# Sketch attention and a squared-relu layer on one core: the first batch's order, the loads of v, and what stands behind x on the queue

## The chip, the core and the metric

The kernel runs on one core of a Trainium2 chip. The core has a matrix engine (TensorE, PE in the profile, its weight loads PEld), VectorE (DVE), ScalarE (ACT), GpSimd (POOL) and SyncE (SP), which issues nearly all the DMAs. The metric is the device time of one execution in microseconds. Beside it stands the span of a profiled execution, from its first to its last instruction.

## The reference

```python
# q, k, v: (4, 4, 1088, 32) float32; S1, S2: (8, 32)
def phi(x):                                  # 64 features: products of two sketches
    a = np.einsum('rd,bhsd->bhsr', S1, x)
    b = np.einsum('rd,bhsd->bhsr', S2, x)
    return np.einsum('bhsi,bhsj->bhsij', a, b).reshape(*x.shape[:-1], 64)
q_p, k_p = phi(q), phi(k)
kv  = np.einsum('bhsf,bhsd->bhfd', k_p, v)   # per head 64 x 32
z   = np.sum(k_p, axis=2)
num = np.einsum('bhsf,bhfd->bhsd', q_p, kv)
den = np.einsum('bhsf,bhf->bhs', q_p, z)[..., None] + 1e-06
x   = (num / den).transpose(0, 2, 1, 3).reshape(4352, 128)
out = np.maximum(x @ w_in, 0)**2 @ w_out     # 128 -> 2048 -> 128, float32 out
```

## The kernel before, in words

The Python code records the instructions of every engine in an order that it fixes itself (a manual schedule); each engine then runs its list in that order, and semaphores make it wait for data and for free buffers.

**Layout.** A batch has 4 heads of 1088 rows. A partition holds 34 consecutive rows of one head: two groups g of 16 rows, and a remainder of 2. A group of a batch is a chunk of 512 tokens for the feed-forward part; there are 8 such chunks and one of 256 tokens for the remainders.

**Feed-forward part.** For each chunk there are 16 blocks: `first_product` (L938) multiplies x, turned (xT, f16), with 128 columns of w_in into a tile pg; relu and square go over VectorE and ScalarE, or ScalarE and POOL (gt, g2); `block` (L1026) multiplies g2 with w_out, adding up in a tile po. The first product is made three blocks ahead. pg has two buffers, so the next pg waits until the relu of the one before last has read it. `first_two` (L968) makes the first two blocks of the first chunk by hand. A finished po is turned, scaled by beta and stored in four pieces by SP (L918).

**Attention.** Rows of k and q are turned in squares of 32 (`turned`, L242) and multiplied with a block-diagonal sketch matrix w_bd (`proj`, L257); `outer` (L344) forms the 64 features. `KvRows` adds up v and k features (`values`, L433) and, from the two factors, the sums z (`factor_sums`, L389); `turn` and `place` (L479, L487) and `own_sums` (L409, L416) spread both over a block-diagonal kvbd. `numerators` (L257, tile nd) multiplies turned q features with kvbd; `normalize` divides, scales each token by its largest value, and keeps the scale for beta. xT comes either over TensorE (x_ps) or, where there is time, over DRAM: SP writes x (L643), waits until it has landed, and reads it back in four pieces (L649).

**The first batch** is written out by hand from L1035 to the end of the setup: seven idle products, which keep TensorE active, the sketch's turn s_ps, four small idle products, then projections, features, sums, values, numerators, normalisation and the first products.

**The later batches** run as generators (`batch_gen`) that are advanced between blocks; a counter of blocks (`now`) and planned costs of VectorE and POOL decide when each continues. For them the features of q come from factors that go over DRAM: `factors_gen` issues q_one (L299), two q_two (L304), and, when these have landed, the two loads of f (L313, L316); POOL multiplies them (phF, L326), and nd waits for phF. `chunk_of` sends beta over DRAM too: SP writes it (L663) and, when it has landed, reads it as beta_t (L664). SP is one queue: a DMA that waits holds up all that stand behind it.

**Loads.** SP issues, in this order, the two k groups of the first batch, k's remainder, q's first group, v by head (four loads of 128 KB over 128 partitions), q's second group, v's remainder (v_rm, two loads, L131), then the weights and the second batch. S1 and S2 come from ScalarE's queue.

Of the kernel before, what the change touches and what calls it, by code (L numbers as in the profile page):

```python
# [8 lines left out]
F32 = mybir.dt.float32  # L9
# [12 lines left out]
def kernel(  # L22
# [24 lines left out]
    VONE = H * 8 * D  # L47
# [33 lines left out]
    for b in range(B):  # L81
        for x, tag in ((k_sb, "k_sb"), (q_sb, "q_sb")):
            x[b] = cpool.tile([128, NM * D], F32, name=f"{tag}{b}")
        v_sb[b] = cpool.tile([128, VONE + D], F32, name=f"v_sb{b}")
    for r in range(2):
        v_rm[r] = cpool.tile([128, H * D + D], F32, name=f"v_rm{r}")
# [33 lines left out]
    def load_v(b, h):  # L120
        sp.dma_start(  # L121
            v_sb[b][:, 256 * h : 256 * h + 256],
            bass.AP(
                v.tensor,
                v.offset + (b * H + h) * S * D,
                [[NM * D, 32], [8 * D, 4], [1, 8 * D]],
            ),
        )

    def load_v_rest(b, i):  # L130
        sp.dma_start(  # L131
            _v(v_rm[b // 2], 0, [[D, H], [1, D]], 64 * (b % 2) + 32 * i, 32),
            bass.AP(
                v.tensor,
                v.offset + (b * H * S + 32 + i) * D,
                [[NM * D, 32], [S * D, H], [1, D]],
            ),
        )
# [26 lines left out]
    load_k(0, 1)  # L165
    load_rest(k_sb[0], k, 0)
    load_q(0, 0)
    for h in range(H):
        load_v(0, h)
    load_q(0, 1)  # L170
    for i in range(2):
        load_v_rest(0, i)
# [7 lines left out]
    for i in range(2):  # L180
        load_v_rest(1, i)
# [14 lines left out]
    for h in range(H):  # L196
        dve.memset(own[32 * h : 32 * h + 32, h : h + 1], 1.0)
    w_bd = cpool.tile([128, H * 16], F32)
# [4 lines left out]
    for i in range(B):  # L203
        (dve if i == 0 else pool).memset(kvbd[i][:], 0.0)
    for b in range(B):
        pool.memset(v_sb[b][:, VONE : VONE + D], 1.0)
    for r in range(2):
        pool.memset(v_rm[r][:, H * D : H * D + D], 1.0)
# [19 lines left out]
    def idle_products(n, w=512):  # L228
        idle_ps = pspool.tile([128, 512], F32, name="idle_ps", tag="po", bufs=2)
        for i in range(n):  # L230
            nc.tensor.matmul(idle_ps[:, 0:w], zero[:, 0:128], zero[:, 0:w])  # L231
# [5 lines left out]
    def turned(x, g, of_q=False):  # L237

        if g < 2:
            xt = apool.tile([128, 512], F32, tag="xt", bufs=6)  # L240
            c0, w = (512 * g, 128) if of_q else (128 * g, 256)
            dve.transpose(  # L242
                xt[:, :] if of_q else _v(xt, 0, [[128, 4], [1, 4], [4, 32]]),
                _v(x, c0, [[32, 4], [w, 4], [1, 32]]),
            )
        else:
            xt = apool.tile([128, 64], F32, tag="xtr", bufs=4)
            if of_q:
                dve.transpose(_v(xt, 0, [[1, 2], [2, 32]]), _v(x, 1024, [[32, 2], [1, 32]]))
            else:  # L250
                dve.transpose(xt[:, :], x[:, 1024:1088])
        return xt
# [32 lines left out]
    def factors_gen(b, qf, w, fs):  # L285


        for g in range(2):


            n, p0 = 2 * w[g], 64 * g
            one = dpool.tile([16, n], F32, name=f"q_one{b}{g}", tag=f"q_one{b}{g}")
# [61 lines left out]
    rest_ab = {}  # L354
    for r in range(2):
        rest_ab[r] = (
            cpool.tile([128, 64], F32, name=f"abr{r}"),
            cpool.tile([128, 256], F32, name=f"phr_k{r}"),
        )

    def proj_rests(xk, b, xqs, qf=None, ps_tag="ms"):


        ab_ps = pspool.tile([128, 128], F32, name="abr_ps", tag=ps_tag, bufs=2)
        p0 = 64 * (b % 2)
        tiled(ab_ps, 0, 64, xk, 0, w_bd[:, :], 64, p0)
        for g, xt in xqs:
            nc.tensor.matmul(ab_ps[64 * g : 64 * g + 64, 64:128], w_bt[:, :], xt[:, 0:64])
        act.copy(
            _v(rest_ab[b // 2][0], 0, [[32, 2], [8, 4], [1, 8]], p0, 64),  # L370
            _v(ab_ps, 0, [[8, 2], [16, 4], [1, 8]], p0, 64),
        )
        for g, _ in xqs:
            act.copy(qf[64 * g : 64 * g + 64, 512:576], ab_ps[64 * g : 64 * g + 64, 64:128])
        return ab_ps

    def outer_rest(b, eng, a=None):
        p0 = 64 * (b % 2)
        ab, ph = rest_ab[b // 2]
        eng.tensor_tensor(  # L380
            out=_v(ph, 0, [[64, 4], [8, 8], [1, 8]], p0, 64),
            in0=_v(ab if a is None else a, 0, [[8 if a is None else 16, 4], [1, 8], [0, 8]], p0, 64),
            in1=_v(ab, 32, [[8, 4], [0, 8], [1, 8]], p0, 64),
            op=mult,
        )

    def factor_sums(ps, c0, ab, a0, a1, w, p0, n, first, last):

        nc.tensor.matmul(  # L389
            ps[32 * w : 32 * w + 32, c0 : c0 + 32],  # L390
            ab[p0 : p0 + n, a0 : a0 + 32],
            ab[p0 : p0 + n, a0 + a1 : a0 + a1 + 32],
# [30 lines left out]
    class KvRows:  # L423
# [3 lines left out]
        def __init__(self, b, abs_=None):  # L427
            self.b, self.abs = b, abs_
            self.ps = pspool.tile([128, 1024], F32, name="kvr_ps", tag="nd", bufs=1)

        def values(self, ph, c0, vt, v0, v1, p0, n, first, last):
            for h in range(H):
                nc.tensor.matmul(  # L433
                    self.ps[32 * h : 32 * h + 32, 0:64],
                    vt[p0 : p0 + n, v0 + v1 * h : v0 + v1 * h + 32],
                    ph[p0 : p0 + n, c0 + 64 * h : c0 + 64 * h + 64],
# [4 lines left out]
        def tile(self, ph, g, t, last=False):  # L441
            self.values(
                ph, 256 * t, v_sb[self.b], D * (4 * g + t), 256, 0, 128, g + t == 0, last
            )

        def rest(self, last=False):
            r, p0 = self.b // 2, 64 * (self.b % 2)
            self.values(rest_ab[r][1], 0, v_rm[r], 0, D, p0, 64, False, last)

        def rest_sums(self):  # L450
            factor_sums(
                self.ps, 512, rest_ab[self.b // 2][0], 0, 32, 0, 64 * (self.b % 2), 64, False, True
            )
# [5 lines left out]
        def keep_sums(self):  # L459
            self.sums = apool.tile([128, 32], F32, name="kvz", tag="kvz")  # L460
            act.copy(self.sums[:, :], self.ps[:, 512:544])

        def products(self, phs):
            for g in range(2):
                for t in range(4):
                    self.tile(phs[g], g, t)
                for t in range(4):
                    factor_sums(
                        self.ps, 512, self.abs, 128 * g + 32 * t, 256, t, 0, 128,
                        g == 0, g == 1 and t > 0,  # L470
                    )
            self.rest(True)
# [19 lines left out]
        def spread(self):  # L492
# [4 lines left out]
            own_sums(self.b, t_ps, 64)  # L497
# [34 lines left out]
    def normalize_first(nds, xT):  # L532


        (den, rden, top, rtop, rs), (_, mp, _, beta) = norm_tiles()
        xs = apool.tile([128, 512], F16, tag="xs")
        for i, nd in enumerate(nds):
# [10 lines left out]
        dve.tensor_tensor(out=rtop[:, :], in0=top[:, :], in1=rden[:, :], op=mult)  # L548

        mm, rm = (_v(nds[1], 144 + 8 * x, [[1, 4]]) for x in range(2))  # L550
        dve.tensor_reduce(
            out=mm, in_=_v(rtop, 0, [[4, 4], [1, 4]]),
            axis=AX, op=amax, apply_absolute_value=True,
        )
        dve.tensor_scalar(
            out=mp[:, :], in0=mm, scalar1=1.0, scalar2=1.0 / 1024.0, op0=add, op1=mult,
        )
        dve.reciprocal(rm, mp[:, :])
        dve.tensor_tensor(
            out=_v(rs, 0, [[4, 4], [1, 4]]),  # L560
            in0=_v(rden, 0, [[4, 4], [1, 4]]),
            in1=_v(nds[1], 152, [[1, 4], [0, 4]]),
            op=mult,
# [8 lines left out]
        yield  # L572
        pool.tensor_tensor(out=beta[:, :], in0=mp[:, :], in1=mp[:, :], op=mult)
# [13 lines left out]
    def normalize(nd, T, xT, col, chunk):  # L587
# [59 lines left out]
        yield 3, 0  # L647
# [32 lines left out]
    nd_taken = [False]  # L680
    ms_until = [0]
# [73 lines left out]
    def batch_gen(b):  # L755
# [55 lines left out]
        kv.spread()  # L811
# [223 lines left out]
    idle_products(7)  # L1035
    s_ps = pspool.tile([128, 16], F32, name="s_ps", tag="nd", bufs=1)
    nc.tensor.transpose(s_ps[:, :], s_nat[:, :], iden[0:16, 0:16])
    idle_products(4, 128)
    xk = [turned(k_sb[0], 0)]
# [5 lines left out]
    )  # L1045
    for x in range(2):
# [5 lines left out]
    pk = [proj(xk[0], "pg"), proj(xk[1], "pg")]  # L1052
    phk = [ph_tile("ph_k", 3) for g in range(2)]
    phq = ph_tile("ph_q", 2)
    xkr = turned(k_sb[0], 2)
    xq = turned(q_sb[0], 0, True)
    for g in range(2):
        outer(phk[g], pk[g][1], 0, 2, dve, pk[g][0])
        outer(phk[g], pk[g][1], 2, 2, pool)
    pq = proj(xq, "po")  # L1060
    pkr = proj_rests(xkr, 0, [])
    kv0 = KvRows(0)
    for g in range(2):
        for t in range(4):
            factor_sums(kv0.ps, 512, pk[g][1], 32 * t, 128, t, 0, 128, g == 0, g == 1 and t > 0)
# [9 lines left out]
    pick_sums(zt_ps, 0, kv0.sums)  # L1075
    for t in range(4):
        kv0.tile(phk[1], 1, t)
    own_sums(0, zt_ps, 0)
    xq1 = turned(q_sb[0], 1, True)
# [17 lines left out]
    kv0.rest(True)  # L1097
    kv0.keep_rows()
    pqT = [turned_half(phq, 0, (act, act))]
# [3 lines left out]
    pqT.append(turned_half(phq, 2, (act, dve)))  # L1103
# [5 lines left out]
    pq1 = proj(xq1, "pg")  # L1109
    phq1 = ph_tile("ph_q", 2)  # L1110
    xT0 = apool.tile([128, 512], F16, name="xT", tag="xT", bufs=3)
    norm = normalize_first(nd0, xT0)
    next(norm)
    for t0 in (0, 2):
        outer(phq1, pq1[1], t0, 2, pool)
# [4 lines left out]
    idle_products(4)  # L1120
    chunk_of(0, 0, xT0, next(norm))
    first_two()
    pqT = [turned_half(phq1, 0, (act, dve))]
# [10 lines left out]
    def second_group():  # L1134
        pqT.append(turned_half(phq1, 2, (act, dve)))
        yield 1, 0
# [6 lines left out]
    lanes.append([second_group(), 1, 1])  # L1143
    add_work(*(batch_gen(b) for b in range(1, B)))
    later = []
    for b in range(2, B):
# [4 lines left out]
        later += [(n + 6 + i, load_v_rest, (b, i)) for i in range(2)]  # L1151
# [40 lines left out]
```

## Time and profile before

| what | value |
|---|---|
| three runs | 196.22, 196.79, 197.50 us; median 196.79 |
| the profiled execution | 196.73 us, span 194.8 us, granted TensorE clock 1.000 |
| TensorE busy | 185.4 us (95% of the span) |
| VectorE, ScalarE, POOL busy | 119.6, 108.2, 71.1 us |
| first idle product | 1.19 us |
| first values (L433) | 8.69 us |
| first pg (L968) | 18.10 us |
| DMA, main queue | 22.86 MB, 45.2% of 16 engines' span |

A line of the timeline reads: start in us from the span's start, length in us, engine, line, operation, output<-input, shapes, count, and in brackets how long the engine was idle before it and what ended that. A q behind an engine's name (SPq) means its queue of DMA issues. A line of the chain of work that ended last reads: start, length, what. `issue` is time in which an engine waited for nothing that the profile shows.

### The profile page before, as it was taken

Reading aid. Unit: us, or ns where it says so; the run is one execution under the profiler, and the core shown is the slowest. Engines: PE = TensorE matmul, PEld = TensorE weight load, DVE = VectorE, ACT = ScalarE, POOL = GpSimd, SP = SyncE. Lnnn points to the kernel's source line nnn. Section 1 sums busy time; section 2 is a strip of 40 time slices with the busy share of each in tenths; the row PEclk is TensorE's granted clock in tenths of the full one; section 3 lists DMA queues with packets and bytes.
Section 4 is the critical chain, followed back from the end, with each engine's and each line's share of the span. In section 5 each row is a group of like instructions: output and inputs, shape, how many; then the busy total and the mean of one; then the engine's idle time right before and its main releaser. Section 6 shows DMA issues by size and latency. Waiting matters only on the chain.

```text
span 194.8 us, 3746 instructions
## 1 busy us (share of the span) xinstructions
PE 185.4 (95%) x1380; PEld 97.2 (50%) x1380; DVE 119.6 (61%) x272; ACT 108.2 (56%) x212; POOL 71.1 (36%) x91
## 2 busy tenths in 40 slices
PE   7985999999999999999999999999999999999992
PEld 2763445454545454545454455554454444444791
DVE  4956495556487848455877545567558664644671
ACT  3235659655466755544766655457646565456570
POOL 3604122645236229242370654542524222522200
PEclk9999999999999999999999999999999999999999
DMA  6799380298913837649130349199100411300021
GB/s 170 212 347 313 107 298 25 59 242 279 228 16 108 253 69 177 192 94 280 27 54 1 52 96 263 42 227 231 29 3 0 84 30 13 54 0 2 5 52 27
DMA packets 37826, 23.17 MB, mean 119 GB/s; under 512 B 27888, under 2 KB 33264, under 8 KB 37808
## 3 DMA queue, kind: packets, MB, share of 16 engines
q1 hardware_dynamic: 37568, 22.86, 45.2%
q8 instruction: 11, 0.18, 0.4%
q14 instruction: 7, 0.06, 0.2%
q10 hardware_dynamic: 240, 0.07, 0.2%
HBM read 16.26 MB, written 6.67 MB: 118 GB/s over the span
## 4 chain that ended last, share of the span: by engine, by line
PE 89%; SPq 3%; DMA 2%; issue 2%; ACT 2%; DVE 1%; DVEq 0%
PE po L1026 56%; PE pg L938 16%; PE nd L257 4%; PE kvr_ps L433 2%; DMA v_rm<-in_v_dram 2%; PE po L985 2%; PE po_r L985 2%; PE ab_ps L257 2%; PE ab_ps L276 1%; SPq L121 1%; PE t_ps L1085 1%; PE idle_ps L231 1%; SPq L105 1%; SPq L95 0%; ACT phTh L74 0%
## 5 line engine op out<-in xcount | busy, mean ns | idle before, releaser
L1026 PE MATMUL po<-g,w_o 128*128 128x512 f32 x256 | 130.7, 592 | 0.1
L955 DVE TENSOR_SCALAR gt<-pg 128x512 f32<-128x512 f32 (+1 forms) x105 | 67.5, 647 | 50.8 <-PE pg L938 42.9
L958 ACT ACTIVATE g<-gt 128x512 f32<-128x512 f32 (+1 forms) x105 | 62.5, 597 | 60.8 <-DVE gt L955 58.8
L1026 PEld LDWEIGHTS po<-g,w_o 128*128 128x128 f32 x256 | 48.5, 191 | 39.7 <-issue 19.7
L938 PE MATMUL pg<-xT,w_in 128*128 128x512 f16 x126 | 47.7, 380 | 1.0 <-DVE own_z L409 0.8
L946 POOL TENSOR_TENSOR g<-gt 128x512 f32<-128x512 f32 x22 | 22.9, 1039 | 70.1 <-ACT gt L945 70.1
L938 PEld LDWEIGHTS <-w_in 128*128 128x128 f16 x142 | 13.9, 98 | 28.1 <-issue 27.1
L326 POOL TENSOR_TENSOR phF<-f,f 128x576 f32<-128x576 f32 (+1 forms) x12 | 16.1, 1364 | 10.7 <-DMA f<-q_two 10.7
L344 POOL TENSOR_TENSOR ph_k<-ab 128x512 f32<-128x512 f32 x14 | 14.5, 1068 | 8.9 <-ACT ab L282 7.7
L945 ACT ACTIVATE gt<-pg 128x512 f32<-128x512 f32 x22 | 12.8, 581 | 0.1
L911 POOL TENSOR_TENSOR o_sb<-oT,beta_t 128x512 f32<-128x512 f32 x8 | 8.4, 1048 | 9.7 <-DVE oT L906 4.0
L952 ACT ACTIVATE g<-gt 128x512 f32<-128x512 f32 x15 | 9.4, 630 | 0.5
L242 DVE STREAM_TRANSPOSE xt<-k_sb 128x512 f32<-128x512 f32 x8 | 8.3, 1106 | 1.4 <-DMA k_sb<-in_k_dram 1.4
L257 PEld LDWEIGHTS nd<-kvbd,phF 128*64 128x64 f32 x208 | 6.9, 137 | 4.5 <-issue 3.8
L951 ACT ACTIVATE gt<-pg 128x512 f32<-128x512 f32 x15 | 8.8, 586 | 0.0
L906 DVE STREAM_TRANSPOSE oT<-po 128x512 f32<-128x512 f32 x8 | 5.7, 717 | 4.8 <-PE po L1026 4.6
L257 PE MATMUL nd<-kvbd,phF 128*64 128x66 f32 x208 | 7.7, 224 | 0.0
L231 PE MATMUL idle_ps<-zero 128*128 128x512 f16 (+1 forms) x15 | 4.8, 477 | 2.8 <-issue 1.6
L257 PEld LDWEIGHTS ab_ps<-w_bd,xt 128*64 128x64 f32 x160 | 6.7, 155 | 1.5 <-issue 0.9
L257 PE MATMUL ab_ps<-w_bd,xt 128*64 128x64 f32 x160 | 6.8, 241 | 0.0
L985 PE MATMUL po<-w_o,g 128*128 128x128 f32 x32 | 6.2, 278 | 0.0
L985 PE MATMUL po_r<-w_o,g 128*128 128x128 f32 x32 | 6.0, 275 | 0.0
(120 smaller groups left out, 132.8 us busy)
## 6 DMA issues: line engine op xcount, KB each, us to landing
q_two<-qf SPq DMA_DIRECT2D x8, 288.0 KB
f<-q_one SPq DMA_DIRECT2D x4, 576.0 KB
f<-q_two SPq DMA_DIRECT2D x4, 576.0 KB
v_sb<-in_v_dram SPq DMA_DIRECT2D x16, 128.0 KB
out_dram<-o_sb SPq DMA_DIRECT2D x32, 64.0 KB
k_sb<-in_k_dram SPq DMA_DIRECT2D x3, 544.0 KB
q_sb<-in_q_dram SPq DMA_DIRECT2D x3, 544.0 KB
w_in<-in_moe_w_in_dram SPq DMA_DIRECT2D x2, 512.0 KB
```

Source lines behind the costliest of these rows:

```text
L257: nc.tensor.matmul(out_ps[p0 + c : p0 + c + z, c0 : c0 + w], lhsT[:, l0 + c : l0 + c + z], rhs)
L326: pool.tensor_tensor(out=ph[:, c], in0=fs[g][0][:, c], in1=fs[g][1][:, c], op=mult)
L344: eng.tensor_tensor(out=_v(ph, 256 * t0, [[64, 4 * m], [8, 8], [1, 8]]), in0=_v(ab if a is None else a, c0, [[n, 4 * m], [1, 8], [0, 8]]), ...
L938: nc.tensor.matmul(pg[:, 0:nt], w_in[:, 128 * c : 128 * c + 128], xT[:, 0:nt])
L945: act.activation(gt[:, 0:nt], pg[:, 0:nt], Relu)
L946: pool.tensor_tensor(out=g2[:, 0:nt], in0=gt[:, 0:nt], in1=gt[:, 0:nt], op=mult)
L951: act.activation(gt[:, 0:nt], pg[:, 0:nt], Relu)
L952: act.activation(g2[:, 0:nt], gt[:, 0:nt], Square)
L955: dve.tensor_scalar(out=gt[:, 0:nt], in0=pg[:, 0:nt], scalar1=0.0, scalar2=None, op0=amax)
L958: act.activation(g2[:, 0:nt], gt[:, 0:nt], Square)
L985: nc.tensor.matmul(po[r][:, 0:128], g2[:, 128 * r : 128 * r + 128], w_o[:, 128 * c : 128 * c + 128], start=c == 0, stop=c == NC - 1,)
L1026: nc.tensor.matmul(po[0][:, 0:nt], w_o[:, 128 * c : 128 * c + 128], g2[:, 0:nt], start=(c == 0), stop=(c == NC - 1),)
```

## The change

- SP's first loads go k, k, q's first group, k's remainder, v, v's remainder, q's second group. Each load of v now fills 32 partitions (a quarter of the rows of all four heads) and not one head's columns in 128, to match a new order of the rows: the turn of k writes without stride.
- The sketch's matrix w_bd is put ahead of the first turn; the idle products are arranged anew, 6 in front of s_ps, 2 behind it, one behind each of the first two projections; the four small ones go, and four in the middle of the normalisation become two in f32 (each two passes).
- k's remainder is turned after the features of k and q's turn. The sums z of the first batch have a PSUM tile of their own.
- Of the first two evictions of turned q features VectorE takes one; of the next two it takes none. The casts of w_in stand ahead of the normalisation.
- The first normalisation takes the larger of 1 and the largest value (one column of ones), where it added 1 before, and loses one instruction.
- The second group of the first batch is projected behind `first_two`; its features, turns and numerators follow later in the stream.
- The remainder's tiles exist once per batch, cleared by POOL, and its products run over 128 partitions, half of them zero, where they ran over 64.
- In later batches `own_sums` comes at least one block later than the rest of `spread`; factors wait until a pending x has been read back, and that read is planned two blocks after the write instead of three.

```diff
-    def load_v(b, h):
-        sp.dma_start(
-            v_sb[b][:, 256 * h : 256 * h + 256],
+    def load_v(b, m, eng=sp):
+        eng.dma_start(
+            v_sb[b][32 * m : 32 * m + 32, :],
             bass.AP(
                 v.tensor,
-                v.offset + (b * H + h) * S * D,
-                [[NM * D, 32], [8 * D, 4], [1, 8 * D]],
+                v.offset + (b * H * S + 8 * m) * D,
+                [[NM * D, 32], [S * D, H], [1, 8 * D]],
             ),
         )
...
     load_k(0, 0)
     load_k(0, 1)
+    load_q(0, 0)
     load_rest(k_sb[0], k, 0)
-    load_q(0, 0)
-    for h in range(H):
-        load_v(0, h)
+    for m in range(4):
+        load_v(0, m)
+    for i in range(2):
+        load_v_rest(0, i, sp)
     load_q(0, 1)
-    for i in range(2):
-        load_v_rest(0, i)
...
+    def clear_rest(b):
+        p0 = 64 - 64 * (b % 2)
+        for t in (v_rm[b], *rest_ab[b]):
+            pool.memset(t[p0 : p0 + 64, :], 0.0)
...
+            if slow:
+                nc.tensor.matmul(idle_ps[:, :], zero_w[:, :], _v(zero_w, 0, [[0, 512]]))
...
-            dve.transpose(
-                xt[:, :] if of_q else _v(xt, 0, [[128, 4], [1, 4], [4, 32]]),
-                _v(x, c0, [[32, 4], [w, 4], [1, 32]]),
-            )
+            dve.transpose(xt[:, :], _v(x, c0, [[32, 4], [w, 4], [1, 32]]))
...
             n, p0 = 2 * w[g], 64 * g
+            while x_due[0]:
+                yield 1, 0
...
             for g in range(2):
                 for t in range(4):
                     self.tile(phs[g], g, t)
+            self.rest()
+            for g in range(2):
                 for t in range(4):
                     factor_sums(
...
-        dve.tensor_scalar(
-            out=mp[:, :], in0=mm, scalar1=1.0, scalar2=1.0 / 1024.0, op0=add, op1=mult,
-        )
-        dve.reciprocal(rm, mp[:, :])
-        dve.tensor_tensor(
+
+        dve.reciprocal(_v(nds[1], 152, [[1, 4]]), mm[:, :])
+        dve.scalar_tensor_tensor(
             out=_v(rs, 0, [[4, 4], [1, 4]]),
             in0=_v(rden, 0, [[4, 4], [1, 4]]),
+            scalar=1024.0,
             in1=_v(nds[1], 152, [[1, 4], [0, 4]]),
...
-        yield 3, 0
+        x_due[0] += 1
+        yield 2, 0
+        x_due[0] -= 1
         for i in range(4):
             sp.dma_start(
...
-        kv.spread()
+        t_ps = kv.spread()
+        yield 1, 0
+        yield from dve_ready(1.0)
+        own_sums(b, t_ps, 64)
+        dve_time(0.6)
...
-    idle_products(7)
+    idle_products(6)
     s_ps = pspool.tile([128, 16], F32, name="s_ps", tag="nd", bufs=1)
     nc.tensor.transpose(s_ps[:, :], s_nat[:, :], iden[0:16, 0:16])
-    idle_products(4, 128)
-    xk = [turned(k_sb[0], 0)]
+    idle_products(2)
     dve.tensor_tensor(
         out=_v(w_bd, 0, [[16, H], [1, 16]]),
...
+    xk = [turned(k_sb[0], 0)]
...
-    pk = [proj(xk[0], "pg"), proj(xk[1], "pg")]
+    pk = [proj(xk[0], "pg")]
+    idle_products(1)
+    pk.append(proj(xk[1], "pg"))
+    idle_products(1)
...
-    xkr = turned(k_sb[0], 2)
     xq = turned(q_sb[0], 0, True)
+    pq = proj(xq, "po")
     for g in range(2):
         outer(phk[g], pk[g][1], 0, 2, dve, pk[g][0])
         outer(phk[g], pk[g][1], 2, 2, pool)
-    pq = proj(xq, "po")
+    xkr = turned(k_sb[0], 2)
     pkr = proj_rests(xkr, 0, [])
-    kv0 = KvRows(0)
+    kv0 = KvRows(0, None, pspool.tile([128, 32], F32, name="kvz_ps", tag="pg", bufs=2))
...
-    pqT = [turned_half(phq, 0, (act, act))]
+    pqT = [turned_half(phq, 0, (act, dve))]
+    xq1 = turned(q_sb[0], 1, True)
...
-    pqT.append(turned_half(phq, 2, (act, dve)))
+    pqT.append(turned_half(phq, 2, (act, act)))
...
-    pq1 = proj(xq1, "pg")
-    phq1 = ph_tile("ph_q", 2)
+    for c in range(2):
+        act.copy(
+            w_in[:, 512 * c : 512 * c + 512], w_in32[:, 512 * c : 512 * c + 512]
+        )
+    idle_products(2, True)
     xT0 = apool.tile([128, 512], F16, name="xT", tag="xT", bufs=3)
     norm = normalize_first(nd0, xT0)
     next(norm)
+    chunk_of(0, 0, xT0, next(norm))
+    for b in range(1, B):
+        pool.memset(kvbd[b][:], 0.0)
+        clear_rest(b)
+    first_two()
+    pq1 = proj(xq1, "ms")
+    phq1 = ph_tile("ph_q", 2)
     for t0 in (0, 2):
         outer(phq1, pq1[1], t0, 2, pool)
-    for c in range(2):
-        act.copy(
-            w_in[:, 512 * c : 512 * c + 512], w_in32[:, 512 * c : 512 * c + 512]
-        )
-    idle_products(4)
-    chunk_of(0, 0, xT0, next(norm))
-    first_two()
-    pqT = [turned_half(phq1, 0, (act, dve))]
```

## The prediction

> **What bounds the kernel now.** The profiled execution took 196.73 us (span 194.8 us and 1.93 us around it); the median of three runs is 196.79 us, so the sum below is made against 196.73. I read the page first, then the chain of work that ended last, then the timeline of the first 26 us engine by engine, then the queue of SyncE (SP).
>
> The page gives TensorE 185.4 us of 194.8 (95%); by the table of stretches it is busy for the whole of 20 to 180 us, except 0.04 us in 25:30 and 0.84 us in 80:100. So the time is TensorE's fixed stream plus what passes before the stream is full, and only gaps of TensorE are worth anything. The chain shows those of the first batch (start, us, what):
>
> ```profile
> 6.59 4.08 DMA v_rm<-in_v_dram
> 10.81 0.32 PE kvr_ps L433 x8
> ...
> 14.66 1.61 issue
> 16.27 1.02 PE idle_ps L231 x4
> 17.30 0.34 PE x_ps L577 x4
> 18.10 0.61 PE pg L968 x2
> ...
> 128.25 1.09 PE nd L257 x32
> ```
>
> See the wait for the two remainder rows of v until 10.81; the 1.61 us in which TensorE waited for nothing that the profile shows; and the first product of the feed-forward part at 18.10. The last line is used below. The pause comes one weight load behind 220 pairs of weight load and matmul (counted off the timeline). The page has a queue that carries code:
>
> ```profile
> q8 instruction: 11, 0.18, 0.4%
> ```
>
> 0.18 MB in 11 packets is 16 KB each; TensorE has 2760 weight loads and matmuls, 251 a packet. So I read the pause as code that had not landed, in a stretch where the DMA engines are full (share 1.02 in 10:15 and 15:20).
>
> The later gap, from the timeline:
>
> ```profile
> 78.38 2.27 SPq L649 DMA_DIRECT2D xT<-x  x4
> 83.26 0.38 PE L938 MATMUL pg<-xT,w_in 128*128 128x512 f16 x1 [0.84 <-DVE own_z L409]
> ```
>
> This pg is the first of the fourth chunk. Its xT was issued at 78.38, behind the next batch's factor transfers; own_z is VectorE work that pg does not read, so I put the 0.84 us down to the landing of xT.
>
> **The change part by part.**
>
> *Start to the values.* Rows: a strided turn against an unstrided one, and the instruction that is dropped from the normalisation.
>
> ```profile
> 4.96 1.05 DVE L242 STREAM_TRANSPOSE xt<-k_sb 128x512 f32<-128x512 f32 x1
> 6.00 0.71 DVE L242 STREAM_TRANSPOSE xt<-q_sb 128x512 f32<-128x512 f32 x1
> 15.48 0.16 DVE L555 TENSOR_SCALAR mp<-nd_b 128x4 f32<-128x4 f32 x1
> ```
>
> One idle product less (0.43: seven in 3.17) puts s_ps at 3.86 instead of 4.28, w_bd at 4.2 to 4.4, the turns (0.71 each) at 4.3, 4.95 and 5.6. The first projection starts at 5.07 (5.09 before). Then an idle product stands between the projections: 0.43 while products are slow (before 6.9 us a pair of projection matmuls takes 0.10, after it 0.06), 0.21 later. Second projection 6.40 (6.07), third 7.37 (6.87). ScalarE's copies, then the DVE products follow: ph_k 7.76 (7.58), then the k remainder's turn, 0.2, now behind both: its projection 8.62 (7.43), the copy, the last factor sum 9.2 (8.17). The values no longer wait for the copy of the sums (another PSUM tile): 9.3 (8.69), and run 0.65, 0.35 and 0.65 with the picks between: remainder products ready at 10.58. The remainder of v is issued one 256 KB load and 0.59 us of SP earlier, so its landing, 10.7, falls to about 9 and binds no more. Gain here 10.81 - 10.58 = 0.23.
>
> *To the numerators.* VectorE takes one of the first two evictions (it waits for ScalarE's half, as at L76 before), so ScalarE's two placings end at 12.22 instead of 12.72 and its next two copies at 13.03, against 13.57 for the last half before. nd_b ends at 13.66 (14.20): gain so far 0.54. The second group's turn, 0.71 on VectorE, runs at 12.3 to 13.0 in front of the first reduction (nd ends 13.0): no cost; it would cost what it is late by.
>
> *Normalisation.* Eleven small steps from 14.24 to 16.86 lose L555 with its gap: 0.20. The fused step is bounded by 0.16 (tensor_scalar) and 0.25 (reciprocal), I take 0.17 as the product it replaces. xs is ready at 16.12: gain 0.74.
>
> *The pause.* Up to and with first_two the new order has 213 pairs; the limit of 220 now falls into pq1, behind them. The four idle products (1.02) gave way to two f32 ones, four passes of 0.43 (row of L1026), 13.7 to 15.4, over before xs's first half at 15.8. x_ps follows at once: pg at 16.97 instead of 18.10, gain 1.13. If pq1 must wait for code, cover is there: TensorE then waits for gt until 18.0.
>
> *Second group and clears.* Projection (0.63) moves into that wait; its first four turns (0.43) from a gap into the stream, a cost. POOL's 12 clears stand between beta (15.4) and the first g2 (18.2): 0.17 for 132 columns, 0.08 for 32, so at most 2.0 us; 0.8 spare, and past that each microsecond delays po. Without the strided turns (1.07 each, VectorE 4.97 of 5 us in 25:30) and with gt ahead of the evictions, the sixth po ends at 27.1 instead of 28.56, and the lead when the second batch is projected is about 1.55. Bounds 1.0 and 2.0.
>
> *Loads of v by m'.* Each now writes 32 partitions, 128 KB as before, 0.6 us of SP. No such transfer is in the trace; nearest are the old v loads (landed by 8.69, when the values began with no wait for them) and the remainder's 32 partitions (4.08 us from issue under load). [...]
>
> *x before factors.* The fourth chunk's gap goes: 0.84. But each queue behind it waits. SP now takes, in order: x, four xT, beta, beta_t, and only then q_one. The trace has this very order, with the next issue at 159.66, 7.06 us behind x; and the last batch's chain as it is:
>
> ```profile
> 111.22 0.44 SPq L643 DMA_DIRECT2D x<-xsT  x1
> 113.78 0.51 SPq L299 DMA_DIRECT2D q_one<-qf  x1
> 118.85 0.36 SPq L316 DMA_DIRECT2D f<-q_two  x1
> ...
> 152.60 0.44 SPq L643 DMA_DIRECT2D x<-xsT  x1
> 154.58 2.21 SPq L649 DMA_DIRECT2D xT<-x  x4
> 156.89 0.55 SPq L663 DMA_DIRECT2D beta<-beta  x1
> 159.06 0.51 SPq L664 DMA_DIRECT2D beta_t<-beta  x1
> 159.66 0.43 SPq L643 DMA_DIRECT2D x<-xsT  x1
> ```
>
> ```profile
> 123.94 2.50 POOL L326 TENSOR_TENSOR phF<-f,f 128x512 f32<-128x512 f32 x2 [4.77 <-DMA f<-q_two]
> ```
>
> In the last batch q_one moves from 113.78 to 111.22 + 7.06 = 118.28. From q_one to phF it was 10.16 here with xT in between, 9.19 in the batch before (72.38 to 81.57); xT is gone by then, so 9.2: phF 127.5 to 130.0. nd stands at the same block as before and began at 128.25: TensorE waits 1.75 (1.0 if the chain takes 8.5, 2.7 if 10.16). POOL's g2 behind phF is not due before nd. Third batch: x at 69.0, q_one 76.1, phF ends 87.8; nd, one block nearer to its projection, at 89.87 - 1.07 - 0.84 = 87.96: 0 (up to 0.85). Second batch: these chunks go over TensorE, no change.
>
> *Rest.* The third chunk's x_ps stands one block nearer to its first pg; xT was copied by 58.33 and would be due at 58.35: 0.1. The padded remainder streams the same columns, the later own_sums and the 0.35 us saved per k turn lie beside a full TensorE: nothing.
>
> Sum: -1.55 - 0.84 + 1.75 + 0.1 = -0.54; 196.73 - 0.54 = **196.2 us**.
>
> **The rivals.**
> - *The factors are in time*: the wait at nd stays under 0.3. For it: the 1.8 us between phF (126.44) and nd before, and less traffic. Against: the 4.5 us that q_one moves. 196.73 - 1.55 - 0.84 + 0.2 = 194.5.
> - *Slower: the factor chain at its long price.* With 10.16 from q_one to phF in both batches, nd waits 2.7 and 0.85: -2.39 + 3.55 + 0.1 = +1.26, 198.0. It decides the sign once the two waits pass 2.3 together. For it: 9.9 in the second batch (36.34 to 46.24); against: 9.19 in the third, at this size.
> - *The pause is not about the count*: then it again follows the numerators, 13.7 to 15.3, the f32 products end at 17.0, pg comes 0.85 later: 197.0. For it: the profile names no releaser. [...]
> [...]
>
> **How the numbers follow.** Forecast 0.45, factors in time 0.30, long chain 0.13, pause elsewhere 0.07, late v 0.05. The forecast's own range is 195.4 to 197.2 (bounds of the lead and of the wait). Eight in ten: from 194.3, most of the first rival, to 198.1, most of the second. One per cent, about what a measurement of this kernel can tell from no change, is 194.8 and 198.8 here: faster 0.26 of the first rival and 0.05 of the forecast, 0.31; slower 0.08 (the long chain with a short lead); the same 0.61.
>
> **What would show it.** Right: first pg near 17.0, no pause ahead of x_ps, remainder products at 10.6 with no wait for v_rm, no gap at the fourth chunk's first pg, q_one of the last batch some 7 us behind x, and TensorE idle 1 to 2.7 us ahead of that batch's first nd, ended by POOL's phF. Wrong: no such idle time, or values that wait for v, or the pause of 1.6 us ahead of pg again.

## The result, and the profile after

The changed kernel is slower: median 200.66 us of 20 executions (197.72 to 204.63) against 196.92 us of 20 for the kernel before, ratio 1.0142, 95% interval 1.0105 to 1.0178; a later comparison of the same two kernels, on another occasion, gave 1.0244 (1.0201 to 1.0287). I had forecast 196.2 us. The ratio leaves out executions more than 1.5% above the fastest of the same kernel, here nine of the changed kernel's twenty, so 1.0142 is the low side: the medians of all twenty stand at 1.019. The one profile of the changed kernel that shows a granted clock of 0.95 throughout (e1) is read for nothing below.

The profiled execution is the fastest of the 20: 197.72 us, span 195.9. The starts of the same product po in both timelines show where it won and lost (us; the right columns are a second profile of the same kernel, e9 below, at 202.54 us):

| place | before | after | difference | e9 | difference |
|---|---|---|---|---|---|
| first po | 19.92 | 18.97 | -0.96 | 19.16 | -0.76 |
| ahead of the fourth chunk | 75.10 | 73.92 | -1.18 | 74.12 | -0.98 |
| behind its first pg | 86.70 | 84.49 | -2.21 | 84.69 | -2.01 |
| behind the third batch's second nd | 102.43 | 101.38 | -1.05 | 102.44 | +0.01 |
| ahead of the last batch's first nd | 124.00 | 122.82 | -1.18 | 123.88 | -0.12 |
| behind it | 133.79 | 134.88 | +1.09 | 139.77 | +5.98 |

From the last row on, both stay apart by the same amount to the end. The lead of the start (1.2 here) and the gap at the fourth chunk (1.03) are there; two waits take back 1.16 and 2.27 (2.02, spread over both nd of the third batch, and 6.10 in e9).

The chain of work that ended last, profiled execution of the changed kernel (start, us, what). The start went nearly as worked out: no wait for v_rm, no `issue` ahead of x_ps, first pg at 17.14.

```profile
10.35 0.70 PE kvr_ps L441 x40
...
16.05 0.30 PE x_ps L586 x2
...
17.14 0.61 PE pg L984 x2
...
97.13 2.78 POOL phF L340 x2
99.95 1.27 PE nd L269 x32
...
128.06 1.27 POOL phF L340
129.38 1.04 PE nd L269 x28
```

The chain now runs through POOL's phF twice, ahead of the third batch's second nd and of the last batch's first. The timeline of TensorE, changed kernel: the first pg of the fourth chunk at 80.48 has no idle time in front of it (0.84 before), and the two nd have.

```profile
80.48 0.39 PE L954 MATMUL pg<-xT,w_in 128*128 128x512 f16 x1
```

```profile
99.95 1.21 PE L269 MATMUL nd<-kvbd,phF 128*64 128x66 f32 x31 [0.94 <-POOL phF L340]
```

```profile
128.16 0.34 PE L269 MATMUL nd<-kvbd,phF 128*64 128x66 f32 x4 [1.10 <-POOL phF L340]
129.38 1.04 PE L269 MATMUL nd<-kvbd,phF 128*64 128x66 f32 x28 [0.88 <-POOL phF L340]
```

SP's queue in the changed kernel, around the third batch's second factors and the last batch's first:

```profile
80.74 0.39 SPq L652 DMA_DIRECT2D x<-xsT  x1
85.25 2.27 SPq L660 DMA_DIRECT2D xT_rem<-x  x4
87.56 0.50 SPq L313 DMA_DIRECT2D q_one<-qf  x1
```

```profile
110.18 0.45 SPq L652 DMA_DIRECT2D x<-xsT  x1
112.27 2.22 SPq L660 DMA_DIRECT2D xT<-x  x4
114.59 0.55 SPq L674 DMA_DIRECT2D beta<-beta  x1
116.98 0.51 SPq L675 DMA_DIRECT2D beta_t<-beta  x1
117.58 0.50 SPq L313 DMA_DIRECT2D q_one<-qf  x1
```

The second is the order that I had summed: q_one is 7.40 us behind x (7.06 forecast). The first I had not seen: the remainder's x holds the factors too, and q_one goes out at 87.56 where it went out at 84.02.

What is not in this profile is the excess of the other executions: the median lies 2.9 us above it. Their granted clocks tell a first thing: of the 20, seven ran at 1.000 (median 198.91 us), ten at 0.991 or 0.992 (median 201.1), three lower. The kernel before has such executions too, but fewer: of the 51 that stand beside the experiments, 15 have 0.991 or less (median 198.2) and 36 have 0.995 or more (196.6).

### The profile page after: what moved, and what is told of

Same layout as the page of the kernel before. It is cut to its first block, busy times and chain, and to the rows that moved or that the text cites. A ratio compares the mean times of both kernels' runs of the same rounds, so it can differ in the third digit from the quotient of the medians.

```text
span 195.9 us, 3760 instructions
## 1 busy us (share of the span) xinstructions
PE 186.5 (95%) x1379; PEld 96.9 (49%) x1379; DVE 117.4 (60%) x271; ACT 108.2 (55%) x212; POOL 73.3 (37%) x100
## 4 chain that ended last, share of the span: by engine, by line
PE 72%; DMA 14%; SPq 5%; DVE 3%; POOL 2%; issue 1%; ACT 1%; DVEq 0%; POOLq 0%
PE po L1042 42%; PE pg L954 12%; DMA q_two<-qf 8%; PE nd L269 4%; PE ab_ps L269 2%; DMA x<-xsT 2%; SPq L660 2%; POOL phF L340 2%; PE idle_ps L246 2%; DMA f<-q_two 2%; PE po L1001 2%; PE po_r L1001 2%; PE kvr_ps L441 1%; PE ab_ps L288 1%; SPq L318 1%
## 5 line engine op out<-in xcount | busy, mean ns | idle before, releaser
L246 PE MATMUL idle_ps<-zero 128*128 128x512 f16 x10 | 4.6, 580 | 1.2 <-DVE own L193 1.2
L257 DVE STREAM_TRANSPOSE xt<-q_sb 128x512 f32<-128x512 f32 x8 | 5.4, 693 | 0.5 <-DMA q_sb<-in_q_dram 0.4
```

## The experiments

Differences in the diffs are to the changed kernel unless the text says otherwise.

**e1, the changed kernel again.**

> The changed kernel as it is, to see another of its executions. In the profiled one (197.72 us) TensorE idled 0.94 us ahead of the third batch's second nd and 1.98 us ahead of the last batch's first nd, both ended by POOL's phF; most of its other executions took 199 to 203 us. Theory A (the factors of q, issued behind x and its read back, are late, and how late is set by landings that differ from one execution to the next): the same two waits, together 3 to 8 us, first pg again near 17.1, and TensorE's lead before the third batch about 1.2 us as in that execution; 199 to 202 us. Rival B (TensorE is granted less clock in most executions, by the records 0.975 to 0.992): the two waits stay at 2.9 together, products of 0.43 us become longer in some stretch, and the time is made there. Rival C (the start is what differs): first pg at 18 to 20.

Median 202.22 us of six, ratio 1.0244. The slow result stands; which of A, B and C makes it, this run alone does not show, since its profile is the one at a clock of 0.95.

**e2, no hold.**

```diff
-            while x_due[0]:
-                yield 1, 0
...
-        x_due[0] += 1
-        yield 2, 0
-        x_due[0] -= 1
+        yield 3, 0
```

> The changed kernel with the factors of q issued as in the kernel before (they do not wait for a pending x, and x is read back three blocks after its write). Theory A: no wait ahead of the two nd; the lead of the start (1.2 us at the second batch's end) stays and the gap at the fourth chunk's first pg comes back (0.84 to 2 us, since x is written no earlier against the stream): 195.0 to 196.5 us, faster than the kernel before by about 1. Rival B or C: 199 to 202 us as the changed kernel.

Median 199.36 us, ratio 1.0122 (1.0073 to 1.0170): between the theories, and mine missed by 3 us. The two waits at nd are gone, the gap at the fourth chunk's first pg is back, and larger. TensorE's timeline, e2:

```profile
84.87 0.58 PE L950 MATMUL pg<-xT,w_in 128*128 128x512 f16 x1 [3.24 <-DMA xT<-x]
85.25 1.91 PE L1038 MATMUL po<-g,w_o 128*128 128x512 f32 x2
```

The wait is 3.24 us, and the po behind it takes 1.91 us for its two passes, where it takes 1.02 elsewhere. The table of stretches (stretch, length, then PE, PEld, DVE, ACT, POOL busy, and after them the granted clock, DMA share, GB/s) shows why:

```profile
80.71:84.12 3.41, 0.92 (x74) 0.81 (x62) 0.00 (x0) 0.52 (x3) 0.99 (x1) 1.00 0.43 130
84.12:87.54 3.42, 2.67 (x12) 1.11 (x13) 0.69 (x1) 0.63 (x1) 1.49 (x2) 0.50 0.15 30
87.54:90.95 3.41, 3.41 (x15) 1.75 (x12) 1.47 (x5) 1.05 (x3) 0.00 (x0) 0.50 0.96 218
90.95:94.36 3.41, 3.41 (x11) 1.43 (x9) 2.04 (x4) 1.77 (x3) 1.55 (x2) 1.00 1.00 296
```

Behind the wait the clock is halved for 6.83 us (84.12 to 90.95), so this wait cost more than its 3.24 us; my sum had no such term.

**e3, the kernel before with the hold alone.** Diff to the kernel before:

```diff
             n, p0 = 2 * w[g], 64 * g
+            while x_due[0]:
+                yield 1, 0
...
-        yield 3, 0
+        x_due[0] += 1
+        yield 2, 0
+        x_due[0] -= 1
```

> The kernel before with only the new order behind x (factors wait until a pending x has been read back, x read two blocks after its write). Theory A: the gap at the fourth chunk's first pg goes (0.84 to 1.05 us), the waits at the third batch's second nd and the last batch's first nd come, 1.2 and 2.3 us of stream in the one profile seen and more in other executions: 199 to 203 us. Rival B or C (the slow part comes from the new start or from the clock): 195.5 to 197.5 us.

Median 203.43 us, ratio 1.0329 (1.0277 to 1.0381): theory A. The order behind x costs 6 us on the old start, more than the whole change. Its profile has a third form of the loss, on POOL and TensorE:

```profile
86.68 2.50 POOL L328 TENSOR_TENSOR phF<-f,f 128x512 f32<-128x512 f32 x2 [8.85 <-DMA f<-q_two]
89.13 1.05 POOL L951 TENSOR_TENSOR g<-gt 128x512 f32<-128x512 f32 x1
```

```profile
90.23 1.13 PE L1031 MATMUL po<-g,w_o 128*128 128x512 f32 x2 [2.12 <-POOL g L951]
```

phF waits for its factors at the head of POOL's queue, the square g2 of a block stands behind it, and a po waits 2.12 us for that: the late factors stop the feed-forward part itself.

**e4, the 449th instruction.**

```diff
-    idle_products(2, True)
+    idle_small(24)          # 24 products of 64 columns, f16
```

> The changed kernel with 24 short idle products (64 columns, f16) in place of the two long ones behind the numerators, so that TensorE meets its 449th weight load or matmul among them and not behind the first two pg. Theory A (code that has not landed stops TensorE there, whatever stands there): some 16 of the short products run at once, then a pause of about 1.6 us with no releaser, TensorE goes on at about 16.2, and x_ps is late by at most 0.3 us. Rival (the pause in the kernel before follows the numerators or the drop of load and not the count): all 24 run together, with no pause among them.

Theory A, to the instruction (the one execution took 203.91 us). TensorE's timeline, e4, by shape:

```profile
14.02 0.64 PE L251 MATMUL idle_ps<-zero 128*128 128x64 f16 x16
16.31 0.39 PE L251 MATMUL idle_ps<-zero 128*128 128x64 f16 x8 [1.65 <-issue]
```

Sixteen run, then nothing for 1.65 us, then the other eight. So the pause belongs to the count and not to the numerators: in this trace as in those of the kernel before, e3, e6 (0.44 us there), e8 and e10 it stands behind the 449th recorded instruction of TensorE, whatever that is. The code packet ran from 13.82 to 14.96 us in this trace, from 13.55 to 14.72 in the kernel before; TensorE went on 1.35 and 1.55 us after its end. In the changed kernel it ended at 14.49 and TensorE came there at 17.8, with no pause. That the packet is the code that TensorE waits for is inferred from the count and from this order; the profile names no releaser. And here as well a halved clock follows (3.41 us from 18.25):

```profile
14.84:18.25 3.41, 1.47 (x20) 0.86 (x21) 2.16 (x9) 0.49 (x2) 2.43 (x14) 1.00 1.11 306
18.25:21.66 3.41, 3.41 (x21) 1.71 (x18) 2.27 (x4) 2.64 (x6) 2.85 (x3) 0.50 1.12 212
```

**e5 and e6, neither wait.** e5 is e2 with, and e6 the kernel before with:

```diff
-        if 16 * chunk - now[0] < 12:
+        if 16 * chunk - now[0] < 14:
```

> The changed kernel with the factors issued as before (no hold) and x of the fourth and seventh chunk turned on TensorE (threshold of 12 blocks made 14), so that neither x nor the factors wait on DRAM there. Theory A (the lead of the start, 1.2 us in the one profile, is lost again at the first wait for DRAM: xT with no hold, factors with it; and a pause of 1.6 to 3.2 us halves the granted clock for 3.4 or 6.5 us behind it, as seen in three traces of the first group): no gap at the fourth chunk's first pg, no halved clock, two turns of 0.22 us and their place on TensorE paid: 196.9 - 1.2 - 0.9 + 0.5 = 195.3, within 194.8 to 196.5 since the lead was 0 to 1.2 in the traces so far. Rival (the new start itself costs): 197.5 us or more.

> The kernel before with x of the fourth and seventh chunk turned on TensorE, its own start. Theory A: the gap of 0.84 us goes and 0.5 is paid, 196.9 - 0.84 + 0.5 = 196.5 (195.8 to 197.0); the difference to the kernel with the new start on the same chip is what the start is worth by itself, 0.3 to 1.2 us. Rival: no difference between the two, or this one faster.

e5: 196.63 us, ratio 0.9975 (0.9947 to 1.0002). e6: 197.55 us, ratio 1.0011 (0.9982 to 1.0040). With the DRAM waits out of the way the new start is worth 0.9 us between the medians, the size of its lead; each came out about 1 us over what I had added up, just outside the range that I had given for it. The profile of e5 shows why the lead is less sure than the profiled execution made it seem: the first pg is at 18.32, since TensorE's clock was still half at 9 us (16 projection products take 1.12 us here, 0.69 in the profile after):

```profile
6.91 1.12 PE L269 MATMUL ab_ps<-w_bd,xt 128*64 128x64 f32 x16
...
18.32 0.59 PE L980 MATMUL pg<-xT,w_in 128*128 128x512 f16 x2 [0.48 <-DVE xT L75]
```

In the profiles of the changed start the full clock came at 3.9 (e7) to 10.4 us (e5), and the first pg at 17.14 to 18.32, once (e7) at 19.49. In four profiles of the old start (the kernel before, e3, e6, e10) it came at 17.49 to 18.10. So the 1.18 us in the table set the earliest profile of the new start against the latest of the old: by the medians of these profiles (without e4, whose start is another) the 31st block starts 0.65 us earlier. In the old start the wait for v_rm until 10.81 stood behind the projections and could take in such a delay; that was not tested by itself.

**e7, betas behind the factors.**

```diff
         beta = yield from norm
+        if 16 * (2 * b + g) - now[0] > 7:
+            yield 2, 0
         chunk_of(b, g, xT, beta)
```

> The changed kernel with the hold, but beta and its read back come two blocks later where there is time, so that SP takes x, xT and then at once the factors. My sum had q_one 7.06 us behind x, of which the two betas and the landing between them are 3.4. Theory A: q_one some 2 to 4.5 us behind x, phF in time, no wait ahead of the third batch's second nd nor ahead of the last batch's first nd, and no halved clock behind them: 195.5 to 197.5 us against 200 to 202 for the changed kernel. Rival (the xT reads themselves or the traffic delay the factors): still 199 or more, with TensorE waiting for phF.

Theory A, and better than forecast: 194.93 us, ratio 0.9887 (0.9845 to 0.9930), faster than both kernels. SP's queue, e7, last batch:

```profile
111.69 0.39 SPq L652 DMA_DIRECT2D x<-xsT  x1
113.72 2.22 SPq L660 DMA_DIRECT2D xT<-x  x4
116.03 0.50 SPq L313 DMA_DIRECT2D q_one<-qf  x1
```

q_one is 4.34 us behind x, and the third batch's second q_one, at 84.69, now goes ahead of the remainder's x (90.56). There is no gap at the fourth chunk and no wait at either nd. The profiled execution is the slowest of the seven (197.03 us): its clock was halved once, in the start, from 10.68 to 14.10, and from its first values to its first pg it took 9.23 us, where the changed kernel's profile has 7.79. The other six ran at a clock of 0.995 or more.

The edit moves a second thing: the nd stand later in the stream, the third batch's second by two blocks and the last batch's first by three (behind 83 blocks and not 80). So phF has more time as well. In this trace its two halves ended at 127.47 and 128.69; at the old place, by the kernel before (128.18, the same stream to 0.01 us there), TensorE would have waited some 0.2 us (an estimate) and not 1.98. Most of the cure is the earlier factors, the rest is the later nd.

**e8, made waits.** Diff to the kernel before (the small products add nothing to the output):

```diff
+        if now[0] in gap_at:        # blocks 20, 64, 70, 96, 104, 110, 116, 122
+            gap(gap_at[now[0]])     # n = 1 to 8
...
+    def gap(n):
+        for last in (False, True):
+            g_ps = pspool.tile([128, 512], F32, name="gap_ps", tag="ms", bufs=2)
+            nc.tensor.matmul(g_ps[:, 0:64], zero[:, 0:128], gap_sb[:, 0:64])
+            if not last:
+                act.copy(gap_sb[:, 0:64], g_ps[:, 0:64])
+                for _ in range(n):
+                    pool.tensor_copy(out=gap_sb[:, :], in_=gap_sb[:, :])
```

> The kernel before with eight made waits: behind certain blocks TensorE waits for ScalarE's copy of a small product and one to eight POOL copies behind it, some 1 to 4 us; the small products add nothing to the output. Theory A (a pause halves the clock afterwards, and which ones do depends on length and on where the pause falls): pauses under about 1 us leave the granted clock at 1.00, those of 3 us and more are followed by 3.4 us or more at 0.50, and between 1.5 and 3 us some are and some are not; each such stretch costs some 1.7 us over the pause. Rival (the halved clock in the first group comes from something else, such as power or the chip): the clock stays at 1.00 behind all eight.

Theory A (one execution, 235.8 us). The waits were 1.31, 2.29, 2.31, 3.22, 3.49, 3.42, 4.26 and 4.35 us; the clock stayed at 1.00 behind the first two and fell to 0.50 behind the other six, for 3.41 us three times and for 6.83 three times. The second and the third are of one length, so the length alone did not decide:

```profile
109.80 0.19 PE L1152 MATMUL gap_ps<-gap_sb,zero 128*128 128x64 f16 x1 [2.29 <-POOL gap_sb L1156]
...
121.05 0.19 PE L1152 MATMUL gap_ps<-gap_sb,zero 128*128 128x64 f16 x1 [2.31 <-POOL gap_sb L1156]
```

In each trace the changes of the clock lie whole multiples of 3.413 us apart (in the kernel before it is full from 6.93 to 194.67 us, 55 times 3.413; in e4 the halved stretches begin at 18.25 and 134.30, 34 times). Cut by that grid, the stretches of e8 read (PE busy is the first number behind the length, the clock the third from the end):

```profile
104.94:108.35 3.41, 2.57 (x8) 1.05 (x7) 2.40 (x9) 2.18 (x5) 0.44 (x1) 1.00 0.00 0
108.35:111.76 3.41, 1.96 (x7) 0.98 (x7) 0.83 (x2) 1.23 (x2) 2.51 (x5) 1.00 0.03 5
...
118.59:122.00 3.41, 1.10 (x6) 0.60 (x5) 0.44 (x1) 0.73 (x2) 3.29 (x7) 1.00 0.87 212
122.00:125.42 3.42, 3.42 (x6) 1.48 (x5) 1.22 (x3) 1.26 (x2) 1.67 (x3) 0.50 0.81 236
```

The wait of 2.29 us lies across a boundary, 0.84 in one stretch and 1.45 in the next, and nothing follows; the one of 2.31 lies inside one stretch, which leaves 1.10 us busy of 3.41, and the next stretch is halved.

**e9 and e12, the changed kernel twice more.**

> The changed kernel as it is, one look more, since its median (200.7) lies 3 us above its profiled execution (197.7). Theory A: TensorE waits for phF ahead of the third batch's second nd and the last batch's first nd, about 1 and 2 to 4 us; where a stretch of 3.41 us holds more than about 1.9 us of waiting (1.95 of 3.41 in one trace so far, 1.70 not) the next 3.41 us run at a granted clock of 0.50, 1.7 us more: 199 to 202. Rival (the excess over the profiled execution comes from the start): first pg at 18.5 or later and waits as in the profiled one.

> The same again; expected the same. Both together say how far the wait at the last batch's nd and the halved clock behind it differ from one execution to another.

e9 took 202.54 us, e12 198.60. The first pg is at 17.34 and 17.39 in them: the start does not make the difference, the rival falls. The waits at the last nd are 2.40 and 0.74 us in e9, 1.14 and 0.89 in e12. TensorE's timeline and the stretches of the grid, e9:

```profile
130.53 0.49 PE L269 MATMUL nd<-kvbd,phF 128*64 128x66 f32 x4 [2.40 <-POOL phF L340]
131.75 1.81 PE L269 MATMUL nd<-kvbd,phF 128*64 128x66 f32 x28 [0.74 <-POOL phF L340]
```

```profile
126.82:130.24 3.42, 1.31 (x4) 0.38 (x2) 1.41 (x2) 1.23 (x2) 1.03 (x1) 1.00 0.77 271
130.24:133.65 3.41, 2.39 (x33) 2.07 (x34) 0.00 (x0) 0.00 (x0) 3.41 (x4) 0.50 0.91 224
133.65:137.06 3.41, 3.41 (x6) 1.47 (x6) 2.44 (x9) 1.32 (x3) 0.25 (x2) 0.50 0.71 183
```

and those of the first profile of the same kernel:

```profile
125.34:128.75 3.41, 2.06 (x9) 0.68 (x7) 1.41 (x2) 1.62 (x3) 1.91 (x2) 1.00 0.88 276
128.75:132.16 3.41, 2.78 (x34) 1.84 (x35) 1.34 (x4) 0.65 (x2) 2.58 (x3) 1.00 1.02 301
```

The same wait, 3.14 us in e9 and 1.98 in the first profile, falls across the boundary of the grid in the first profile and leaves 2.06 us busy; in e9 2.11 us of it fall into one stretch, and 6.83 us at half clock follow. By the table at the top this place cost 2.27 us in the one and 6.10 (5.98 + 0.12) in the other.

**e10, the kernel before with x, xT, factors, beta in this order** (the diffs of e3 and e7 together, on the kernel before).

> The kernel before, its own start, with x read back ahead of the factors and beta two blocks later. If the order x, xT, factors, beta is what pays, and the new start only adds its lead (0.9 us by the two runs with x turned on TensorE): no gap at the fourth chunk, no wait for phF: 197.0 - 0.84 to 1.2 = 196.0, with the gain of the variant of the changed kernel (194.9) made of 1.0 from the order and 1.0 from the start. Rival (the new start is worth all of it): 197.0, as the kernel before; or (the order is worth all of it): 195.0.

195.60 us, ratio 0.9963 (0.9932 to 0.9993); the kernel before had 196.39 in this comparison. There is no gap at the fourth chunk and no wait at an nd; these stand two and three blocks later here too. Moving the betas, and with them the nd, takes away the whole loss of e3 (1.0329); against the kernel before, the order x, xT, factors, beta pays about 0.8 us on the old start. e7 against it (0.9887 against 0.9963) puts the new start at 0.8%, e5 against e6 at 0.4%: between 0.7 and 1.5 us.

**e11, the remainder's x does not hold.**

```diff
-        x_due[0] += 1
+        x_due[0] += T > 1
         yield 2, 0
-        x_due[0] -= 1
+        x_due[0] -= T > 1
```

> The changed kernel where the remainder's x no longer holds the factors; whole chunks' x still do, betas stay ahead of the factors. Theory A: the third batch's second q_one goes out 3 us earlier, the wait of 0.94 us at its second nd goes, the wait at the last batch's first nd stays: 0.9 to 1.2 us less than the changed kernel, 199.0 to 200.0. Rival (all of the loss comes from one place, the last batch): no difference, 200.2 or more.

Median 199.66 us, ratio 1.0152 (1.0095 to 1.0208). In its profile the third batch's second q_one goes out at 81.67, the wait at its nd is gone, and the one at the last batch's first nd is there (1.79 and 0.89 us, with 3.41 us at half clock). The place is shown; that it is worth 1 us of the time is not, because the changed kernel's own ratios (1.0142 and 1.0244) lie on both sides of this one.

## Why the prediction was wrong

Point by point, by the terms of its sum:

- *Start, -1.55.* Measured -1.18 in the profiled execution, and that one was lucky: some 0.65 by the medians of the profiles. The single times were close: values at 9.35 (9.3 forecast), x_ps at 16.05 (xs at 16.12), first pg 17.14 (16.97). The sixth po ended at 27.8, not 27.1. From the first pg to there it took 10.64 us, against 10.46 before and 10.13 forecast. The numerators (0.62 twice) and four of the second group's turns (0.44) stand there in both kernels, and the other four turns I had costed; so what I had expected from the missing strided turns and the earlier gt was some 0.5 us too much. What the text lacked altogether is how much the start varies (first pg 17.14 to 18.32, and 19.49 with a halved clock).
- *The pause and the count.* Right: e4 shows the count (449 recorded instructions, for which I had 220 pairs and one), and the rival of 197.0 falls. In the changed kernel TensorE came there 3.3 us behind the packet's end and did not pause; in the kernel before and in e4 it came while the packet ran, and paused for 1.61 and 1.65 us.
- *v by m'.* My sum had no delay for v, and the 0.05 for a late v was an estimate of mine. No run shows a delay: no profile of the changed start has a wait for v or v_rm, and the values began at 9.35 in the profiled execution (9.3 forecast). The form of the load was not tried by itself.
- *The fourth chunk's gap, -0.84.* Right: -1.03.
- *The last batch's nd, +1.75.* The mechanism is right (q_one 7.40 behind x, TensorE idle 1.98 us until POOL's phF), its size 2.27 in that execution, 2.31 in e12 and 6.10 in e9.
- *The third batch.* I looked at its first nd (0 to 0.85; it waits 0 to 0.43) and not at its second, whose q_one the remainder's x holds as well: 1.16 in the profile, and 1.83 (e12) and 2.02 (e9) for both nd together.

The two waits pass 2.3 us together, the point at which my slower rival was to decide the sign. Its reason, a long chain from q_one to phF (10.16), was there in e9 (10.30) and not in the profiled execution (9.26) or e12 (9.38), where the forecast's 9.2 held. In these two it is the wait at the third batch's second nd, which neither the forecast nor the rival had, that turns the sign.

The step that failed is "x before factors", in its price: +1.75 for the last batch and 0 for the third. At full clock the two places cost 3.43 us (the profiled execution) and 4.14 (e12), above all because the remainder's x holds the factors as well; that alone makes a loss out of the gain. And a wait of TensorE was entered as its own length. Where 1.95 us of waiting or more fell into one stretch of the grid, the runs put 3.41 or 6.83 us at half the clock behind it, up to 1.7 or 3.4 us more; with that, the two places cost 8.12 us in e9. The range, to 198.1, had little room for the one and none for the other.

The halved clock fits the spread of the twenty executions: ten at a clock of 0.991 or 0.992, which is one such stretch (half of 3.41 us over 200 is 0.0085), three with more. The median of the ten is 2.2 us above that of the seven at 1.000, somewhat more than the 1.7 us that one such stretch can take; that of the seven is 2.0 us above the kernel before, with no halved clock at all. Where the halved stretch of those thirteen lies is not shown: e9 and e11 have it at the last batch's nd, e7 in the start.

e7 is the counter-test: the same change, with 3 us less between x and q_one (and nd later), has neither of the waits, nor a halved clock behind them, and is 1.1% faster than the kernel before.

What stays open: why the moment of the full clock at the start lies anywhere from 3.9 to 10.4 us (in e2 and e5 stretches with only 0.27 and 0.18 us idle were followed by another one of slow products), and how much of the median each of the two waits makes.

## What to carry to other kernels

Where an edit puts transfers ahead of others on one queue, follow every later item of that queue, the small ones with a landing between them above all: two betas of 2 and 8 KB, with the landing between them, cost this kernel 5 to 7 us (e7's ratio against the changed kernel's two; the nd moved with them), and two blocks of delay for them turned a loss of 1.4 to 2.4% into a gain of 1.1%. Price a wait of the engine that bounds the kernel at its length plus what follows it (here 3.41 or 6.83 us at half the clock, where 1.95 us or more of one stretch of 3.41 were idle), and be wary of a lead: in e2 the lead of the start was lost at the next transfer, where TensorE waited 3.24 us for xT and the kernel before 0.84. One profile is one draw (here it was the fastest of twenty); where a wait lies near the length behind which the clock was halved (1.75 us idle in a stretch was not enough here, 1.95 was), look at several.

## What the runs showed of the hardware that I had not expected

The granted clock of TensorE is 1.00 or 0.50 in these profiles (e1's 0.95 apart), and in them it changes only on a grid of 3.413 us that each execution lays differently (the change to full at the start is at 5.87 in the profiled execution of the changed kernel, at 6.93 in that of the kernel before). Over the stretches of this grid in thirteen traces, from 12 us on: up to 1.75 us idle (e3; 1.61 in the kernel before) left the next stretch at 1.00, 1.95 (e4), 1.97 (e3), 2.11 (e9), 2.14 (e11) and all above made it 0.50. Behind a halved stretch with up to 0.54 us idle (e11) the clock was full again; with 0.75 (e2), 1.03 (e9), 1.17, 1.23 and 1.35 (e8) another halved one followed. In the start, with small products, 1.50 us were once enough (e7), and 0.76 in the first stretch did not keep the clock down (e7).
